# Softmax divisions, first differences and some low words of a fused attention, mix and channel kernel on other engines

## The chip, the cores and the metric

The kernel runs on one core of a Trainium2 chip. The metric is device microseconds for one execution of the whole program, from the first to the last instruction and the little that lies around them. A core has five engines with queues of their own, which meet through semaphores: TensorE (PE in the rows, its weight loads PEld), VectorE (DVE), ScalarE (ACT), GpSimd (POOL) and SyncE (SP), whose queue issues the DMAs here. Each engine takes its instructions strictly in order.

## The reference

Three stages in a chain, for a batch of 4, 576 positions, 8 heads of 64 channels (512 channels together):

```python
# 1 attention, per head: a window of 32 positions (plain, or with a stride of 4)
scores = where(mask, scale * q @ k.T, -1e9)
attn = exp(scores - max(scores));  attn = attn / (sum(attn) + 1e-9)
x = attn @ v
# 2 mix, with x_prev the row before
xk = mu_k * x + (1 - mu_k) * x_prev;  xr = mu_r * x + (1 - mu_r) * x_prev
k = relu(xk @ w_k);  y = sigmoid(xr @ w_r) * ((k * k) @ w_v)
# 3 channel
u = y + U, V mixing of y over positions
out = u + relu(u @ w_ch1) @ w_ch2
```

The weights arrive as 64-bit floats and are turned into 32-bit ones on the chip.

## The kernel before

**Attention** works on units: one unit is a pair of heads, one of two parts of the sequence and one batch element, 32 units in all. The first four units (`attend`) go alone, the other 28 in pairs (`attend2`). A unit has ten or eight windows of 32 queries by 64 keys. Its steps are: TensorE products `qk` (L606, L685) into `psS`; on VectorE mask and maximum (`low`, L546); on ScalarE the exponential with its sum, one instruction for each 64 columns (`exp`, L555); on VectorE the reciprocal of the sums (`inv`, L560 and L561); the division, which is a product with that reciprocal (`norm`, L566), **on GpSimd**, in one instruction for up to five groups of 64 columns; TensorE transposes (L637, L723); on ScalarE the copy `pts` out of PSUM; TensorE products with v (L649, L741); on ScalarE the copy into `x`.

**Mix** goes over eight half batches c = 0 to 7, each with four slices p of 128 channels. For each, `mix` makes the first difference `d` = x minus x of the position before (L356, **on GpSimd**) and from it `xk` (for c = 0) or `m` by one VectorE instruction (L778). For c = 0 the products are plain 32-bit matmuls (`r_row` L837, `k_row` L852, then L821), each of which the trace records twice; from c = 1 on each operand is split into a high word (copy on ScalarE, L361) and a low word (subtraction, L356 on GpSimd or L358 on VectorE), and each product is three fast matmuls (L824 to L826). A tile of a later c is 12 such matmuls; each c has 4 tiles for r, 8 for k and, for v, 4 of twice that length. PSUM has four banks `psM` for these accumulators and four `psS` for attention. The row of `r_row` for slice 3 ends the r sums of c = 0, which `sg` copies on ScalarE take out of the banks before `k_row` can go on.

**The weights of mix**, 20 pieces `wx` of 128x512, are loaded through a pool of four buffers `w`, and each is converted by one ScalarE instruction (L394) and four on VectorE (L395, L396, L398, L401); the last of them frees the buffer for the next load. Later `split_weight` makes `wh` and `wl` of each.

**The order** is not the order of the code. Each step is an `op` with an engine, an estimated duration and its reads and writes; `plan` passes forward and backward over all of them and gives each engine a fixed list. A duration or an engine that changes in one `op` can so move instructions on every engine. Where `plan` sees TensorE idle for over 0.6 us, it puts matmuls on zeros there (L1340), which take time as others do.

**After mix** the channel stage (from about 305 us on, L1058 to L1060 and L1137 to L1139) follows. The change has no instruction in it.

Of the kernel before, what the change touches and what calls it, by code (L numbers as in the profile page):

```python
# [76 lines left out]
FILL, FILL_FROM, FILL_NS, FILL_COLD = 0.6, 600.0, 0.453, 7000.0  # L77
PLAN_PRINT = None
PASSES = 24
EARLIER = {"d": -20}  # L80
RATE = 285.0

# [2 lines left out]
def tile_attention_mix_channel(  # L85
# [44 lines left out]
    def op(eng, ns, fn, r=(), w=(), more=100, lock=False, mode=None, size=0):  # L130

        o = Op()
        o.eng, o.ns, o.fn, o.r, o.w, o.more, o.lock, o.mode, o.size = eng, ns, fn, list(r), list(w), more, lock, mode, size
        ops.append(o)
# [217 lines left out]
    def sub(eng, n, out_, a, b, r, w, psum=False, fr=True):  # L352

        if eng == "POOL":
            t = 165 + 2.14 * n if fr else 110 + 1.93 * n
            op("POOL", t, lambda: nc.gpsimd.tensor_tensor(out=out_(), in0=a(), in1=b(), op=ALU.subtract), r, w, 40, lock=True)  # L356
        else:
            dve(n, lambda: nc.vector.tensor_tensor(out=out_(), in0=a(), in1=b(), op=ALU.subtract), r, w, two=True, psum=psum)  # L358
# [201 lines left out]
        nc.vector.tensor_scalar(sm[:, :n], sm[:, :n], 1e-9, None, op0=ALU.add)  # L560
        nc.vector.reciprocal(sm[:, :n], sm[:, :n])  # L561

    def norm(pr, d, sm, i, n, d_to=None):
        src = pr[:, d : d + n * KW].rearrange("p (w k) -> p w k", k=KW)
        dst = src if d_to is None else pr[:, d_to : d_to + n * KW].rearrange("p (w k) -> p w k", k=KW)
        nc.gpsimd.tensor_tensor(out=dst, in0=src, in1=sm[:, i : i + n].unsqueeze(2).to_broadcast([P, n, KW]), op=ALU.mult)  # L566

    LOW, EXP, NORM = 150, 330, 1.69 * KW

    def x_out(ov, q, part, b):  # L570

# [15 lines left out]
    def attend(u):  # L587
# [34 lines left out]
            for i in range(5):  # L622
                exp(pr(), i * KW, mn(), sm(), i)

        def norms():
            norm(pr(), 4 * KW, sm(), 4, 1, 5 * KW)
            norm(pr(), 0, sm(), 0, 5)

        op("DVE", 6 * LOW, lows, [(x,) for x in sc] + [("cst",)], [(pr,), (mn,)], 170)
        op("ACT", 5 * EXP, exps, [(pr,), (mn,)], [(pr,), (sm,)], 190, mode="exp")  # L630
        op("DVE", 260, lambda: inv(sm(), 5), [(sm,)], [(sm,)], 80, lock=True)
        op("POOL", 360 + 6 * NORM, norms, [(pr,), (sm,)], [(pr,)], 40, lock=True)
        yield

        def tr():
# [23 lines left out]
    def attend2(ua, ub):  # L659
# [33 lines left out]
        for e in range(2):  # L693
            first_, own = (ns - 4, 0) if e else (0, 4)
            base = e * ns * KW

            def lows(e=e, first_=first_, own=own, base=base):
                for i in range(4):
                    low(sc[e](), i * KW, pr(), base + (first_ + i) * KW, mk[i // 2], mn[e](), first_ + i)
                if nw == 10:  # L700
                    for f in range(2):
                        low(sc[f](), (4 + e) * KW, pr(), base + own * KW, mk[2], mn[e](), own, head(f))

            def exps(e=e, base=base):
                for i in range(ns):
                    exp(pr(), base + i * KW, mn[e](), sm[e](), i)

            kp, ks = [(pr, e)], [(sm[e],)]
            op("DVE", (4 + 2 * (ns - 4)) * LOW, lows, [(x,) for x in (sc if nw == 10 else sc[e : e + 1])] + [("cst",)], kp + [(mn[e],)], 170)
            op("ACT", ns * EXP, exps, kp + [(mn[e],)], kp + ks, 190, mode="exp")  # L710
            op("DVE", 260, lambda e=e: inv(sm[e](), ns), ks, ks, 80, lock=True)
            op("POOL", 180 + ns * NORM, lambda e=e, base=base: norm(pr(), base, sm[e](), 0, ns), kp + ks, kp, 40, lock=True)
        yield

        def to(i):
# [48 lines left out]
    def mix(c, p, which):  # L764
# [7 lines left out]
        d, kd = lambda: dt_[p // 2]()[:, p % 2 * HS : (p % 2 + 1) * HS], (dt_[p // 2], p % 2)  # L772
        if (c, p) not in dd:
            dd.add((c, p))
            sub("POOL", HS, d, lambda: x()[:, p, c0 : c0 + HS], xp, kx, [kd], fr=False)
        n = 4 * base + p
        out_, km = (lambda: xk0()[:, n * HS : (n + 1) * HS], (xk0, n)) if c == 0 else half_slot("m")
        dve(HS, lambda: nc.vector.scalar_tensor_tensor(  # L778
            out=out_(), in0=d(), scalar=mu_t[:, col + p : col + p + 1], in1=xp(), op0=ALU.mult, op1=ALU.add),
            kx + [kd, ("mu",)], [km] + ([("turn", "m")] if c else []), two=True)  # L780
        if c > 0:
            at(xk, 8 * base + p, 8 * base + 4 + p, out_, [km], "POOL")


    xk0 = Lazy([P, 8 * HS], F32, "x", "xk0", 2)
# [649 lines left out]
```

## Time and profile before

| | us |
|---|---|
| median of 3 runs | 750.92 (749.88 to 753.05) |
| the profiled execution | 750.69 |
| its span, first to last instruction | 748.8 |
| TensorE busy in the span | 733.4 |
| VectorE, ScalarE, GpSimd busy | 564.4, 393.1, 381.5 |

The prediction is made against the profiled execution: 750.69 us, 0.2 us below the median of the runs, and 1.9 us longer than its span. TensorE was busy for 98% of the span, so the first question is where the other 15.4 us are, and what of its busy time is matmuls on zeros. The views to read are the busy time by stretch, the timeline of TensorE with its waits, and for the other engines the timelines around those waits. In a timeline row the first number is the start, the second how long the row's instructions kept the engine busy from first start to last end, and "x8" their count; in brackets stands the idle time of the engine just before and what ended it.

### The profile page before, as it was taken

The page shows a single profiled execution, that of the slowest core. Times are in us where ns is not written, and L with a number is a line of the kernel's source. Part 1 is how long each engine was busy: PE and PEld are TensorE (multiplying, and loading weights), DVE is VectorE, ACT ScalarE, POOL GpSimd, SP SyncE. Part 2 cuts the span into 40 slices and gives each one's busy share as a digit, 9 for nine tenths or more (in the row PEclk, how much of TensorE's full clock was granted, in tenths as well). Part 3 has the DMA queues.
Part 4 walks back from the last instruction along what each step waited for, and adds up shares of the span by engine and source line. Part 5 has one row for each costly group of instructions (what it writes and reads, how often), then busy time and mean ns, then how long its engine had stood idle before and what let it go on. Part 6 is the DMA issues. An engine that isn't in the chain of part 4 may idle for free.

```text
span 748.8 us, 18318 instructions
## 1 busy us (share of the span) xinstructions
PE 733.4 (98%) x6920; PEld 675.5 (90%) x6920; DVE 564.4 (75%) x1335; ACT 393.1 (53%) x995; POOL 381.5 (51%) x400
## 2 busy tenths in 40 slices
PE   7899989999999999999999999999999999999998
PEld 5677989999999999999999898889888989898886
DVE  5999998899988754875778698785997765675532
ACT  5596785867676746473556345354454433343310
POOL 1332464646554644273766587444877645365500
PEclk9999999999999999999999999999999999999999
DMA  8877327767765550466733262133412212141001
GB/s 318 271 258 257 116 95 235 265 204 263 278 194 185 164 169 15 169 187 206 238 131 120 90 217 75 43 127 127 162 57 85 86 56 85 40 134 67 15 1 56
DMA packets 53223, 109.77 MB, mean 147 GB/s; under 512 B 5648, under 2 KB 15888, under 8 KB 53136
## 3 DMA queue, kind: packets, MB, share of 16 engines
q1 hardware_dynamic: 53136, 108.62, 43.4%
q8 instruction: 54, 0.88, 0.5%
q14 instruction: 33, 0.27, 0.1%
HBM read 86.05 MB, written 22.54 MB: 145 GB/s over the span
## 4 chain that ended last, share of the span: by engine, by line
PE 88%; DVE 5%; DMA 3%; ACT 2%; issue 1%; SPq 0%; POOL 0%; DVEq 0%; ACTq 0%; POOLq 0%
PE psM L824 10%; PE psM L826 10%; PE psM L825 10%; PE psS L1139 9%; PE psS L1137 9%; PE psS L1138 9%; PE psM L1058 8%; PE psM L1060 8%; PE psM L1059 8%; PE psS L741 2%; DMA w<-w1raw 2%; PE psM L821 1%; PE psS L685 1%; DVE wx L401 1%; DVE wx L398 1%; DMA raw<-qk 1%
## 5 line engine op out<-in xcount | busy, mean ns | idle before, releaser
L356 POOL TENSOR_TENSOR cl<-sums,ch 128x512 fp32r<-128x512 f32 x72 | 97.6, 1355 | 91.0 <-ACT ch L361 59.4
L361 ACT ACTIVATE ch<-sums 128x512 fp32r<-128x512 f32 (+1 forms) x104 | 57.7, 563 | 122.5 <-DVE sums L481 113.2
L1137 PE MATMUL psS<-hh,rh 128*128 128x512 f32 (+2 forms) x322 | 119.5, 371 | 0.4 <-ACT hh L1114 0.4
L1139 PE MATMUL psS<-hl,rh 128*128 128x512 f32 (+2 forms) x322 | 119.6, 371 | 0.0
L1138 PE MATMUL psS<-hh,rl 128*128 128x512 f32 (+2 forms) x322 | 119.2, 370 | 0.0
L824 PE MATMUL psM<-xk,wh 128*128 128x288 f32 x336 | 100.9, 300 | 0.0
L825 PE MATMUL psM<-xk,wl 128*128 128x288 f32 x336 | 99.1, 295 | 0.0
L826 PE MATMUL psM<-xk,wh 128*128 128x288 f32 x336 | 98.9, 294 | 0.0
L481 DVE TENSOR_TENSOR sums<-st 128x256 f32<-128x256 f32 (+1 forms) x144 | 86.6, 649 | 7.7 <-POOL cl L356 5.9
L356 POOL TENSOR_TENSOR cl<-st,ch 128x256 fp32r<-128x256 f32 x80 | 65.9, 840 | 48.5 <-PE psM L1060 34.9
L356 POOL TENSOR_TENSOR xk<-m,xk 128x288 fp32r<-128x288 f32 x56 | 52.4, 946 | 41.2 <-ACT xk L361 33.9
L1139 PEld LDWEIGHTS psS<-hl,rh 128*128 128x128 f32 x322 | 60.6, 188 | 11.6 <-DVE hl L1115 0.9
L1137 PEld LDWEIGHTS psS<-hh,rh 128*128 128x128 f32 x322 | 60.7, 188 | 10.4 <-ACT hh L1114 1.2
L1138 PEld LDWEIGHTS psS<-hh,rl 128*128 128x128 f32 x322 | 60.7, 189 | 9.4
L824 PE MATMUL psM<-k2s,wh 128*128 128x288 f32 x224 | 67.7, 302 | 0.0
L825 PE MATMUL psM<-k2s,wl 128*128 128x288 f32 x224 | 66.5, 297 | 0.0
L826 PE MATMUL psM<-k2s,wh 128*128 128x288 f32 x224 | 66.4, 296 | 0.0
L824 PEld LDWEIGHTS psM<-xk,wh 128*128 128x128 f32 x336 | 63.0, 187 | 0.7
L1095 DVE TENSOR_TENSOR ok<-ok,psM 128x256 f32<-128x256 f32 (+1 forms) x96 | 46.4, 504 | 22.4 <-PE psM L1060 20.0
L826 PEld LDWEIGHTS psM<-xk,wh 128*128 128x128 f32 x336 | 63.2, 188 | 0.0
L825 PEld LDWEIGHTS psM<-xk,wl 128*128 128x128 f32 x336 | 63.1, 188 | 0.1
L356 POOL TENSOR_TENSOR k2s<-k,k2s 128x288 fp32r<-128x288 f32 x49 | 43.0, 879 | 35.0 <-ACT k2s L361 32.5
(154 smaller groups left out, 2109.7 us busy)
## 6 DMA issues: line engine op xcount, KB each, us to landing
st<-w2f SPq DMA_DIRECT2D x96, 256.0 KB, 3.0
w<-w2raw SPq DMA_DIRECT2D x32, 512.0 KB, 5.2
w<-w1raw SPq DMA_DIRECT2D x20, 512.0 KB, 5.5
w2f<-w SPq DMA_DIRECT2D x32, 256.0 KB, 3.0
raw<-qk SPq DMA_DIRECT2D x16, 320.0 KB, 6.7
ytmp<-y SPq DMA_DIRECT2D x32, 144.0 KB, 2.2
yb<-ytmp SPq DMA_DIRECT2D x4, 1152.0 KB, 6.4
uf<-us SPq DMA_DIRECT2D x32, 144.0 KB, 1.8
```

The source lines that it names most:

```text
L356: op("POOL", t, lambda: nc.gpsimd.tensor_tensor(out=out_(), in0=a(), in1=b(), op=ALU.subtract), r, w, 40, lock=True)
L361: act(n, lambda: nc.scalar.activation(out_(), in_(), AF.Copy), r, w, psum, strided)
L481: dve(k * Q, lambda: nc.vector.tensor_tensor(out=q(sm_, n, k)(), in0=a(), in1=b(), op=op_), [(s1,), (s2,)], [(sm_, key)], two=True)
L824: nc.tensor.matmul(a, lhsT=wh, rhs=xh, start=start, stop=False)
L825: nc.tensor.matmul(a, lhsT=wl, rhs=xh, start=False, stop=False)
L826: nc.tensor.matmul(a, lhsT=wh, rhs=xl, start=False, stop=stop)
L1058: nc.tensor.matmul(a, lhsT=wh()[:, wi], rhs=xh()[:, ci], start=(k == 0), stop=False)
L1059: nc.tensor.matmul(a, lhsT=wl()[:, wi], rhs=xh()[:, ci], start=False, stop=False)
L1060: nc.tensor.matmul(a, lhsT=wh()[:, wi], rhs=xl()[:, ci], start=False, stop=(k == len(parts) - 1))
L1137: nc.tensor.matmul(a, lhsT=wh, rhs=xh, start=(j == 0 and e == 0), stop=False, skip_group_check=c0 > 0)
L1138: nc.tensor.matmul(a, lhsT=wl, rhs=xh, start=False, stop=False, skip_group_check=c0 > 0)
L1139: nc.tensor.matmul(a, lhsT=wh, rhs=xl, start=False, stop=(j == 7 and e == 1), skip_group_check=c0 > 0)
```

## The change

Three things move. The division of the first four units goes from GpSimd to VectorE (the same two instructions each); that of the other 28 goes to ScalarE, as one instruction for each 64 columns with the reciprocal as its scale (124 instructions in place of 28 on GpSimd). The first differences `d` of half batch 0 go from GpSimd to VectorE (4 instructions; those of the other half batches stay). The low words of `xk` of half batch 1 go from GpSimd to VectorE (8; the others stay).

```diff
+NORM_ENG = ("DVE", "DVE", "ACT", "ACT", "ACT")
+MIX_ENG = ("DVE", "POOL")
+XK_ENG = "DVE"
...
-    def norm(pr, d, sm, i, n, d_to=None):
+    def norm(eng, pr, d, sm, i, n, d_to=None):
+        if eng == "ACT":
+            for w in range(n):
+                to = (d if d_to is None else d_to) + w * KW
+                nc.scalar.activation(
+                    pr[:, to : to + KW], pr[:, d + w * KW : d + (w + 1) * KW], AF.Copy, scale=sm[:, i + w : i + w + 1])
+            return
...
-        nc.gpsimd.tensor_tensor(out=dst, in0=src, in1=sm[:, i : i + n].unsqueeze(2).to_broadcast([P, n, KW]), op=ALU.mult)
+        (nc.vector if eng == "DVE" else nc.gpsimd).tensor_tensor(out=dst, in0=src, in1=sm[:, i : i + n].unsqueeze(2).to_broadcast([P, n, KW]), op=ALU.mult)
...
+    def normed(u, n, k, fn, r, w):
+        eng = NORM_ENG[min(u // 2, len(NORM_ENG) - 1)]
+        if eng == "DVE":
+            op("DVE", 75 * k + 1.04 * n * KW, lambda: fn(eng), r, w, 80, lock=True)
+        elif eng == "POOL":
+            op("POOL", k * 180 + n * NORM, lambda: fn(eng), r, w, 40, lock=True)
+        else:
+            op("ACT", 60 + n * 245, lambda: fn(eng), r, w, 140)
...
-        op("POOL", 360 + 6 * NORM, norms, [(pr,), (sm,)], [(pr,)], 40, lock=True)
+        normed(u, 6, 2, norms, [(pr,), (sm,)], [(pr,)])
...
-            sub("POOL", HS, d, lambda: x()[:, p, c0 : c0 + HS], xp, kx, [kd], fr=False)
+            sub(MIX_ENG[min(c, 1)], HS, d, lambda: x()[:, p, c0 : c0 + HS], xp, kx, [kd], fr=False)
...
-            at(xk, 8 * base + p, 8 * base + 4 + p, out_, [km], "POOL")
+            at(xk, 8 * base + p, 8 * base + 4 + p, out_, [km], XK_ENG if c == 1 else "POOL")
```

`plan` then orders everything anew. In the rows below `pr,sm<-pr,mn` is the exponential, `pts` the copy of transposed scores, `wx<-w` the first step of a weight's conversion, `x` the attention's result.

ScalarE, the first instructions after its table load, before:

```order
L555 ACTIVATE pr,sm<-pr,mn 128x64 x5
L394 ACTIVATE wx<-w_100 128x512
L555 ACTIVATE pr,sm<-pr,mn 128x64 x5
L361 ACTIVATE pts<-psS 128x384
L394 ACTIVATE wx<-w_135 128x512
```

The same place after:

```order
L558 ACTIVATE pr,sm<-pr,mn 128x64 x5
L397 ACTIVATE wx<-w_100 128x512
L364 ACTIVATE pts<-psS 128x384
L558 ACTIVATE pr,sm<-pr,mn 128x64 x5
L364 ACTIVATE x_95<-psS 128x320
L397 ACTIVATE wx<-w_135 128x512
```

The exponentials of the second unit now stand behind `pts` of the first.

TensorE between the row of r for slice 1 and the one for slice 3 (`xk,wx 128x288 x4` is one row of r; `zero` is matmuls on zeros; `pts,raw` the products with v; `raw` qk), before:

```order
L1340 MATMUL psM<-zero 128x224 x5
L837 MATMUL psM<-xk_325,wx 128x288 x4
L649 MATMUL psS<-pts,raw 64x32 x20
L685 MATMUL psS<-raw 32x64 x32
L837 MATMUL psM<-xk_325,wx 128x288 x4
L1340 MATMUL psM<-zero 128x224 x5
L837 MATMUL psM<-xk_325,wx 128x288 x4
```

The same place after:

```order
L1358 MATMUL psM<-zero 128x224 x13
L855 MATMUL psM<-xk_302,wx 128x288 x8
L655 MATMUL psS<-cst_t,pr 128x128 x3
L1358 MATMUL psS<-zero 128x512 x2
L759 MATMUL psS<-pts,raw 64x32 x20
L703 MATMUL psS<-raw 32x64 x32
L1358 MATMUL psM<-zero 128x224 x28
L855 MATMUL psM<-xk_302,wx 128x288 x4
```

The rows of slices 1 and 2 now come ahead of the fourth unit's products with v, and before the last row of r there are 28 matmuls on zeros instead of five.

VectorE after the first reciprocal, before:

```order
L560 TENSOR_SCALAR sm<-sm 128x5
L561 RECIPROCAL sm<-sm 128x5
L546 ISA pr,mn<-psS,cst_t 128x64
L546 ISA mn 128x1
L546 ISA pr,mn<-psS,cst_t 128x64
```

The same place after:

```order
L563 TENSOR_SCALAR sm<-sm 128x5
L564 RECIPROCAL sm<-sm 128x5
L398 TENSOR_SCALAR wx<-wx 128x512
L575 TENSOR_TENSOR pr<-pr,sm 128x64
L575 TENSOR_TENSOR pr<-pr,sm 128x320
L399 TENSOR_SCALAR wx<-wx 128x512
```

The two divisions of the first unit stand inside a weight's conversion, ahead of the second unit's maxima.

## Rows read from the trace of the kernel before

**Rows 1.** By stretch: length; PE, PEld, DVE, ACT, POOL busy; clock, DMA share, GB/s.

```profile
40.00:72.40 32.40, 30.78 (x386) 23.73 (x384) 31.23 (x94) 25.84 (x76) 8.02 (x11) 1.00 0.74 247
...
105.00:700.00 595.00, 593.84 (x5383) 558.83 (x5380) 454.22 (x1010) 311.42 (x755) 338.68 (x346) 1.00 0.44 144
...
106.00:107.00 1.00, 1.00 (x10) 0.99 (x5) 0.89 (x9) 1.00 (x4) 1.00 (x2) 0.50 0.89 233
```

**Rows 2.** Timeline of TensorE from 35 to 75 us: start, busy, instruction.

```profile
35.74 2.21 PE L837 MATMUL psM<-xk,wx 128*128 128x288 f32 x8 [0.49 <-DVE xk L778]
...
42.23 6.57 PE L852 MATMUL psM<-xk,wx 128*128 128x288 f32 x26
...
50.12 7.93 PE L821 MATMUL psM<-xk,wx 128*128 128x288 f32 x32
57.88 0.60 PE L723 MATMUL psS<-cst_t,pr 128*128 128x128 f32 x4
...
59.17 1.14 PE L741 MATMUL psS<-pts,raw 64*64 64x32 f32 x64 [0.22 <-ACT pts L361]
...
61.24 8.03 PE L821 MATMUL psM<-k,wx 128*128 128x288 f32 x32
...
69.88 1.63 PE L821 MATMUL psM<-k,wx 128*128 128x288 f32 x6
72.44 2.91 PE L821 MATMUL psM<-k,wx 128*128 128x288 f32 x11 [0.93 <-DVE wx L401]
```

**Rows 3.** Timeline of TensorE around 102 us.

```profile
101.33 0.29 PE L825 MATMUL psM<-xk,wl 128*128 128x288 f32 x1
101.46 0.29 PE L826 MATMUL psM<-xk,wh 128*128 128x288 f32 x1
103.65 1.37 PE L741 MATMUL psS<-pts,raw 64*64 64x32 f32 x80 [1.90 <-ACT pts L361]
...
106.02 0.61 PE L824 MATMUL psM<-k2s,wh 128*128 128x288 f32 x1
...
108.80 0.29 PE L824 MATMUL psM<-k2s,wh 128*128 128x288 f32 x1
```

**Rows 4.** Timeline of ScalarE, the second unit's exponentials and the first `pts`.

```profile
9.62 0.35 ACT L555 ACTIVATE pr<-pr,mn 128x64 f32<-128x64 f32 x1 [1.15 <-DVE mn L546]
...
11.43 0.49 ACT L361 ACTIVATE pts<-psS 128x384 f32<-128x384 f32 x1
```

**Rows 5.** Timeline of VectorE, second reciprocal and `xk` of slice 3.

```profile
12.71 0.17 DVE L560 TENSOR_SCALAR sm<-sm 128x5 f32<-128x5 f32 x1
...
13.17 0.43 DVE L395 TENSOR_SCALAR wx<-wx 128x512 f32<-128x512 f32 x1
...
15.18 0.23 DVE L546 CUSTOM_DVE_ANT_0 pr<-psS,cst_t 128x64 f32<-128x64 f32 x1 [1.13 <-PE psS L606]
...
35.17 0.51 DVE L778 SCALAR_TENSOR_TENSOR xk<-d,mu_t,x 128x288 f32<-128x288 f32 x1
35.60 0.69 DVE L398 SCALAR_TENSOR_TENSOR wx<-w,wx 128x512 int32<-128x512 int32 x1
```

**Rows 6.** Timeline of VectorE, instructions that lasted longer beside GpSimd's.

```profile
19.88 1.23 DVE L395 TENSOR_SCALAR wx<-wx 128x512 f32<-128x512 f32 x2
...
24.11 0.89 DVE L395 TENSOR_SCALAR wx<-wx 128x512 f32<-128x512 f32 x1
...
26.36 1.09 DVE L401 SCALAR_TENSOR_TENSOR wx<-w,wx 128x512 int32<-128x512 int32 x1
...
51.15 2.37 DVE L398 SCALAR_TENSOR_TENSOR wx<-w,wx 128x512 int32<-128x512 int32 x2
```

**Rows 7.** A line on ScalarE: duration ns min/median/max of copies of 128x160.

```profile
L361 ACT ACTIVATE us<-w x4: 323/334/338, 231.1 to 232.4; 128x160 fp32r<-128x160 f32 x4
```

**Rows 8.** GpSimd's groups up to 72.4 us: busy us, mean ns, idle before.

```profile
L356 POOL TENSOR_TENSOR d<-x 128x288 f32<-128x288 f32 x8 | 7.2, 904 | 16.7 <-ACT x L361 16.7
...
L566 POOL TENSOR_TENSOR pr<-pr,sm 128x320 f32<-128x320 f32 x4 | 3.3, 834 | 0.3
```

More of the change, by code (lines that the diff above doesn't have):

```diff
@@ L623, in exps, with norms @@
                 exp(pr(), i * KW, mn(), sm(), i)
-        def norms():
-            norm(pr(), 4 * KW, sm(), 4, 1, 5 * KW)
-            norm(pr(), 0, sm(), 0, 5)
+        def norms(eng):
+            norm(eng, pr(), 4 * KW, sm(), 4, 1, 5 * KW)
+            norm(eng, pr(), 0, sm(), 0, 5)
         op("DVE", 6 * LOW, lows, [(x,) for x in sc] + [("cst",)], [(pr,), (mn,)], 170)
@@ L711, in attend2 @@
             op("DVE", 260, lambda e=e: inv(sm[e](), ns), ks, ks, 80, lock=True)
-            op("POOL", 180 + ns * NORM, lambda e=e, base=base: norm(pr(), base, sm[e](), 0, ns), kp + ks, kp, 40, lock=True)
+            normed(ua, ns, 1, lambda eng, e=e, base=base: norm(eng, pr(), base, sm[e](), 0, ns), kp + ks, kp)
         yield
```

## The prediction

> **What bounds the kernel now.** I first read the busy time by stretch. From 105 to 700 us TensorE works 593.84 of 595.00 us at the full granted clock [rows 1], and the change takes no instruction off TensorE. So nothing can be gained there; what a change of the other engines can give or take lies before 105 us, or is a wait that it newly makes. Then I read TensorE's timeline from 35 to 75 us [rows 2]: its waits are short, and each ends on an engine that the change touches. Third, the one large wait further on [rows 3]. Fourth, what VectorE and ScalarE do before the last row of r [rows 4, 5], because that row waits for `xk` on VectorE, and VectorE is full: 31.23 of 32.40 us from 40 to 72.4 us [rows 1].
>
> Two places therefore hold what there is to win or lose.
>
> **Place 1, the start.** After the last row of r (35.74 us) TensorE still has room before c = 1. I count it from the time after qk of the fifth and sixth units (42.23 us) [rows 2]: 42.23 + 6.57 = 48.80 to 50.12 is 1.32 us, 57.88 + 0.60 = 58.48 to 59.17 is 0.69, 61.24 + 8.03 = 69.27 to 69.88 is 0.61, 69.88 + 1.63 = 71.51 to 72.44 is 0.93. Some of it is idle time and some matmuls on zeros, and all of it, 3.55 us, could be taken up if TensorE came later. The new order puts three matmuls on zeros into this stretch, 0.45 us as an upper bound from the 0.61 us that seven of them cost above.
>
> **Place 2, the wait at 101.75 us.** TensorE stands 1.90 us for `pts`, which is late on ScalarE [rows 3]. [...] So this place costs 1.90 + 1.18 = 3.1 us.
>
> **The change part by part.**
>
> *Divisions of the first four units on VectorE.* No row shows such a product on VectorE. The nearest is `xk`, 128x288 with two tensors from SBUF: the next instruction starts 35.60 - 35.17 = 0.43 us behind it [rows 5]. For 128x320 that makes 0.48, and for 128x64 I take 0.17, as for the 128x5 instruction [rows 5]: 0.65 us a unit. The bounds are 0.43, if the small one costs nothing, and 0.9, a little more than GpSimd's 0.834 for the large one [rows 8].
>
> *First differences of c = 0 on VectorE.* 128x288 again: 0.43 us each, with 0.51, the whole duration of that row, as upper bound.
>
> *What GpSimd no longer disturbs.* VectorE's instructions last longer beside GpSimd's. Up to the last row of r three places show it: two of L395 in 1.23 us for 0.86, one in 0.89 for 0.43, one L401 in 1.09 for 0.69 [rows 5, 6]. Together 0.37 + 0.46 + 0.40 = 1.23 us, all beside instructions that now leave GpSimd. The lower bound of the relief is these 1.23 us; the upper, that each moved GpSimd instruction gives back its whole time: half of the eight `d`, 3.6, and the large divisions, 3.3 [rows 8], 6.9 us. I take the lower, since it is what the rows show.
>
> [...] The rows above show delays of 0.37 to 0.46 us beside GpSimd instructions of 0.8 to 0.9, so half of that at most. [...]
>
> *The last row of r.* From the second reciprocal (12.71) to the end of `xk` of slice 3 (35.60) VectorE takes 22.89 us now. I counted both orders between these two instructions. The new one has 4 `d` (1.72), 3 divisions (1.95), three more steps of weights (two at 0.62, one at 0.40) and one more reciprocal with its addition (0.40): +5.71. Off go the relief, 1.23, and the idle 1.13 us at 15.18 [rows 5], where VectorE waits for qk of the third unit and will now have work: 22.89 + 5.71 - 2.36 = 26.24 us. The start of the stretch moves too. ScalarE now does `pts` of unit 1 ahead of the second unit's exponentials; `pts` can't end before 11.43 + 0.49 = 11.92, because the transpose stays where it was, and the five exponentials took from 9.62 to about 11.4, 1.75 us [rows 4]. So they end at 13.67, and the reciprocal starts at 13.8 instead of 12.71. `xk` of slice 3 is then there at 13.8 + 26.24 = 40.04, and the last row of r at 40.2 instead of 35.74: 4.45 us later. Queued behind the exponentials on ScalarE are `x` and the second weight, which wait with them; behind the divisions on VectorE are all weights.
>
> *Sum of place 1.* 4.45 late, 3.55 of it taken up, 0.45 of zeros: 1.35 us lost. This needs the last weight to come no later than TensorE. VectorE is 4.45 us late at that row but has done three steps of weights and a reciprocal more, 2.04, so 2.4 us in terms of weights; from there to the last weight the order adds two low words and a reciprocal and takes off one `m`, +0.8, and a pair at 51.15 that took 2.37 us for some 1.3 [rows 6] shows relief of 1.1, with some more at others, 2.4 in all as an estimate. The last weight is so 0.8 us later, inside the 1.35. SP's queue has the same loads in nearly the same places, each freed by the last step of an earlier weight, and follows VectorE.
>
> *Low words of half batch 1 on VectorE.* Eight at 0.43, 3.4 us, two of them before the last weight. VectorE has no room from 72 to 103 us either, but GpSimd's divisions and low words there go at the same time. I count it as nothing for the sum; the cover is this relief, and without it the weights' low words come up to 2.6 us later and TensorE waits so long.
>
> *Divisions of the other 28 units on ScalarE.* 124 instructions. A copy of 128x160 takes 0.334 us [rows 7], one of 64 columns no longer; by columns alone it would be 0.13. I take 0.25, nearer the upper, since part of an instruction's time does not shrink. 124 x 0.25 = 31 us (16 to 41) on an engine with over 350 us idle. TensorE sees it only through `pts`, `k2s` and `rt` behind it in the queue; each group of divisions also waits for VectorE's reciprocal, and these stand behind that wait.
>
> *Place 2 after.* The pair of units that waits at 101.75 is now served earlier: its transposes stand after the third k tile less four products instead of late in the seventh, and VectorE and ScalarE have had less time to fall behind. Stepping through ScalarE's list there, `pts` comes just in time for the 12 matmuls between transposes and products, with 0.3 us to spare, but the next pair's maxima and divisions now stand inside the k tiles, and the last `k2s` comes about 1 us after TensorE wants it at the v tiles. What is left there can be anything from 0 to 3.1 us, or more (third case). I take 2.0, one wait of 1.1 with a short fall of the clock: 1.1 us won.
>
> **Sum.** 750.69 + 1.35 - 1.1 = 750.9 us. Measurements of this kernel can tell about 0.5%, 3.75 us, from no change; this is within it. Its own range is 747.5 to 754.5: the divisions at 0.43 to 0.9 move place 1 by -0.7 to +0.8, `d` up to +0.3, the three others of place 1 by about 1, and place 2 by -2.0 to +1.1.
>
> **The rivals.**
>
> [...] If the relief is half way between 1.23 and 6.9, 4.1 us, the last row of r comes at 37.3, 1.6 late; 1.6 - 3.55 + 0.45 = -1.5. If the wait at 101.75 goes too, -3.1: 746.1 us. For it: GpSimd's busy share before 72 us falls to a fraction. Against: the traced delays are small, and VectorE gets 5.7 us of work. It decides once the relief is over 3 us. That this is faster by more than 0.5% needs both halves.
>
> *ScalarE's queue, slower.* Divisions of eight or ten times 0.25 us stand between `k2s` and `rt` in each round of attention, where TensorE asks for a k tile every 12 x 0.13 = 1.6 us. If ScalarE comes later than the slack, TensorE stands as it does now [rows 3], at 3.1 us a time. It decides from a delay of `pts` beyond those 12 matmuls. Of the 14 rounds, two such waits beside the one in the sum would give 750.69 + 1.35 + 6.2 = 758.2. For it: the divisions wait for VectorE inside the queue. Against: after 105 us TensorE has but 1.16 us of waits now [rows 1], with the same chain over GpSimd.
>
> *Nothing of place 2 changes.* The start is taken up as said and an equal wait stays: 750.69 + 1.35 = 752.0, also no change that can be told.
>
> **Chances.** Forecast 0.50, lock 0.22, queue 0.20, equal wait 0.08. Faster by over 0.5% (below 746.9): the lock and a little of the forecast's lower end, 0.24. Slower (above 754.4): the queue and 0.04 of the forecast, 0.24. Within: 0.52. The range that leaves half of each rival out goes from 745.0 to 757.5.
>
> **What would show it.** Right: the last row of r starts near 40 us with idle time ahead of it despite 28 matmuls on zeros; from 42 to 75 us no wait is left; the first matmul of c = 1 is 1 to 2 us later than now, less the attention products that have moved ahead of it; a division of 128x320 on VectorE takes about 0.48 and one of 64 columns on ScalarE about 0.25 us; near 95 us there is no wait for `pts`, and a short one at the first v tiles of c = 1. Wrong: the row of r near 36 us, VectorE's weights finishing before 72, or several waits of over 1 us between 105 and 300 us that end on ScalarE.

## The result and the profile after

| | before | after |
|---|---|---|
| median of 6 runs, us | 750.40 (749.2 to 753.05) | 754.68 (754.12 to 755.94) |
| ratio, 95% interval | | 1.0056 (1.0038 to 1.0075) |
| span of the profiled execution | 748.8 | 752.1 |
| VectorE, ScalarE, GpSimd busy | 564.4, 393.1, 381.5 | 559.7, 420.4, 343.6 |

The change makes the kernel 4 us slower. GpSimd gave up 37.9 us and ScalarE took 27.3; VectorE is even busy for 4.7 us less. The busy time by stretch, of after (as [rows 1]; columns: stretch, length, then PE, PEld, DVE, ACT, POOL busy with counts, granted clock, DMA share, GB/s), says where the loss is:

```profile
40.00:72.40 32.40, 30.73 (x387) 23.86 (x386) 29.34 (x97) 29.00 (x92) 3.54 (x5) 1.00 0.78 261
105.00:260.00 155.00, 150.69 (x2147) 147.38 (x2146) 131.20 (x411) 120.87 (x389) 69.38 (x82) 1.00 0.62 205
105.00:700.00 595.00, 590.14 (x5310) 555.09 (x5309) 447.81 (x990) 328.75 (x829) 323.02 (x324) 1.00 0.43 141
```

From 105 us on TensorE stands 4.86 us where it stood 1.16 [rows 1], and 4.31 of them lie before 260 us. Its timeline after has these waits (answers to [rows 2, 3]):

```profile
34.05 3.39 PE L1358 MATMUL psM<-zero 128*128 128x224 f32 x28
39.03 2.21 PE L855 MATMUL psM<-xk,wx 128*128 128x288 f32 x8 [1.59 <-DVE xk L796]
...
56.91 2.21 PE L839 MATMUL psM<-xk,wx 128*128 128x288 f32 x8 [1.55 <-ACT rt L899]
...
97.37 1.37 PE L759 MATMUL psS<-pts,raw 64*64 64x32 f32 x80 [0.85 <-ACT pts L364]
...
145.31 0.40 PE L842 MATMUL psM<-k2s,wh 128*128 128x288 f32 x1 [0.41 <-DVE k L904]
...
155.88 1.37 PE L759 MATMUL psS<-pts,raw 64*64 64x32 f32 x80 [1.79 <-ACT pts L364]
...
160.35 0.40 PE L842 MATMUL psM<-k2s,wh 128*128 128x288 f32 x1 [0.70 <-issue]
...
206.35 0.40 PE L842 MATMUL psM<-xk,wh 128*128 128x288 f32 x1 [1.09 <-DVE y L919]
```

The first two places moved as foreseen in kind: the last row of r came late, the wait near 102 us shrank from 1.90 to 0.85 us (now at 97 us), and no half clock (a granted clock of 0.50, as before had [rows 1]) followed: it was 1.00 from 97 to 102 us. All rows from 145 us on are new. A ledger puts sizes to it. At the start of each round of products with v I took the difference in time between the kernels, less 0.133 us for each fast matmul of mix (0.133 is their pitch: in before, ten of them start from 108.80 to 110.00 us) that after had done more; where it had done fewer, the same is added:

```
start, before   start, after   matmuls of c >= 1 done   after is late by
120.52          114.48         240 / 204                -1.24
138.99          134.56         360 / 336                -1.23
154.58          155.88         456 / 456                +1.30
192.31          193.55         696 / 684                +2.84
210.79          214.97         816 / 816                +4.18
228.79          232.16         924 / 924                +3.37
```

So the start and the place near 102 us together won 1.2 us, the stretch from 135 to 215 us lost 5.4, and a wait of 0.59 us that only before has at 213 us (0.8 with its restart) leaves 3.3 to 3.4. Nothing changes after that.

The chain of work that ended last, from the page of before and then of after, shares of the span by engine:

```profile
PE 88%; DVE 5%; DMA 3%; ACT 2%; issue 1%; SPq 0%; POOL 0%; DVEq 0%; ACTq 0%; POOLq 0%
```

```profile
PE 71%; DVE 16%; ACT 6%; DMA 4%; issue 2%; SPq 0%; POOL 0%; DVEq 0%; ACTq 0%
```

Before, the chain ran through TensorE from 103 us nearly to the end. After, it runs from 20 to 206 us through VectorE, ScalarE and transfers; of the 101 us from 105 to 206 us VectorE has 54, transfers 20 and ScalarE 16. So VectorE may set the pace there although it is busy for only 131.2 of 155 us. A chain through many short waits is no proof of that; the experiments test it.

### The profile page after: what moved, and what is told of

It is laid out like the page before. It is cut to its first block, busy times and chain, and to the rows that moved or that the text cites. A ratio compares the mean times of both kernels' runs of the same rounds, so it can differ in the third digit from the quotient of the medians.

```text
span 752.1 us, 18403 instructions
## 1 busy us (share of the span) xinstructions
PE 732.5 (97%) x6934; PEld 674.8 (90%) x6934; DVE 559.7 (74%) x1355; ACT 420.4 (56%) x1119; POOL 343.6 (46%) x352
## 4 chain that ended last, share of the span: by engine, by line
PE 71%; DVE 16%; ACT 6%; DMA 4%; issue 2%; SPq 0%; POOL 0%; DVEq 0%; ACTq 0%
PE psS L1157 9%; PE psS L1155 9%; PE psS L1156 9%; PE psM L1076 8%; PE psM L1078 8%; PE psM L1077 8%; PE psM L842 6%; PE psM L844 5%; PE psM L843 5%; ACT pr L558 1%; DVE pr L549 1%; DVE m L796 1%; DVE wl L361 1%; DVE w L404 1%; DVE w L401 1%
## 5 line engine op out<-in xcount | busy, mean ns | idle before, releaser
L359 POOL TENSOR_TENSOR xk<-m,xk 128x288 fp32r<-128x288 f32 x48 | 43.7, 926 | 68.3 <-ACT xk L364 51.3
L359 POOL TENSOR_TENSOR k2s<-k,k2s 128x288 fp32r<-128x288 f32 x49 | 44.7, 913 | 49.9 <-ACT k2s L364 48.1
```

## The experiments

In all of them `before` ran on the same chip, and a ratio is to it, with its 95% interval.

### The parts alone and in pairs

The three parts of the change were moved one by one. "Start" in the table means the first four units' divisions together with the first differences of c = 0:

| start on VectorE | later divisions on ScalarE | low words on VectorE | ratio |
|---|---|---|---|
| | yes | | 1.0021 (1.0001 to 1.0042) |
| | | yes | 0.9996 (0.9980 to 1.0013) |
| yes | | | 1.0082 (1.0062 to 1.0102) |
| yes | yes | | 0.9993 (0.9977 to 1.0009), again 1.0008 (0.9987 to 1.0029) |
| yes | | yes | 1.0016 (1.0001 to 1.0030) |
| | yes | yes | 1.0097 (1.0072 to 1.0122) |
| yes | yes | yes | 1.0056 (1.0038 to 1.0075), again 1.0059 (1.0039 to 1.0079) |

**Later divisions alone.**

```diff
-NORM_ENG = ("DVE", "DVE", "ACT", "ACT", "ACT")
-MIX_ENG = ("DVE", "POOL")
-XK_ENG = "DVE"
+NORM_ENG = ("POOL", "POOL", "ACT")
+MIX_ENG = ("POOL", "POOL")
+XK_ENG = "POOL"
```

> Only the divisions of the units from the fifth on go to ScalarE; the first four stay on GpSimd, as do the first differences of x and the low words of mixes. Theory (ScalarE's time): the TensorE waits of 4.3 us that the changed kernel shows between 105 and 260 us come from the 27 us more of ScalarE work, so they are here too, near 145 and 155 us above all, while the start costs nothing (last row of r near 35.7 us as before, not 39.0) and the wait near 101 us is as in the changed kernel: about 753.8 us, 1.0045 of before. Rival (low words): the waits come from half batch 1's low words on VectorE; then they are missing here and the kernel is faster than before by the 2.2 us that the place near 101 us gave: about 748.2 us. Rival (order): the waits belong to the one order that was planned for the changed kernel, and this kernel has waits of its own, anywhere from 747 to 756 us, at other places.

751.96 us, 1.0021: neither the 753.8 of the theory nor the 748.2 of the first rival. No engine makes TensorE wait between 105 and 260 us; its 1.6 us of idle time there have no releaser in the trace. So 27 us more on ScalarE do not by themselves make the waits.

**The change without divisions on ScalarE.**

```diff
-NORM_ENG = ("DVE", "DVE", "ACT", "ACT", "ACT")
+NORM_ENG = ("DVE", "DVE", "POOL")
```

> No division on ScalarE: those of the first four units stay on VectorE and the others go back to GpSimd; first differences of x and half batch 1's low words on VectorE as in the changed kernel. Theory (ScalarE's time): no wait beyond 0.6 us between 105 and 260 us; the start costs its 0.9 us; the place near 101 us keeps some wait: 749 to 752 us. Rival (low words): the 4.3 us of waits between 105 and 260 us stay: about 754 us. Rival (order): any time from 748 to 756 us, with the waits at new places.

752.23 us, near the 749 to 752 of the first theory, with waits for an engine of 0.31 and 0.52 us at other places. One wait of 1.88 us, without a releaser, it did not foresee.

**The change without low words on VectorE**, measured twice.

```diff
-XK_ENG = "DVE"
+XK_ENG = "POOL"
```

> The changed kernel with half batch 1's low words of mixes back on GpSimd; divisions and first differences of x stay where the change puts them. The kernel with the divisions of later units on ScalarE alone showed no TensorE wait on an engine between 105 and 260 us. Theory (sum of three parts): the start costs 1 to 1.4 us, the place near 101 us gains 2, and the waits near 145, 155 and 206 us come with the low words and the order that they force; without these words they go: about 751.0 us, 1.001 of before. Rival (ScalarE's time at a full VectorE): the waits stay at 145 and 155 us, since the divisions and the first differences are still there: about 754.5 us, as the changed kernel.

> The changed kernel without its low words on VectorE, once more: 0.9993 of before, 0.998 to 1.001; no TensorE wait for an engine over 0.5 us between 72 and 260 us, as in its first profile. If that profile was a lucky one, waits of 1 us and more appear here.

Both times as fast as before, with 0.3 us of waits for an engine from 72 to 260 us in the first profile, 0.3 in the second. Against the full change the low words cost about 4 us here, their new order included; without the two other parts (second row) they cost nothing.

**The start alone.**

```diff
-NORM_ENG = ("DVE", "DVE", "ACT", "ACT", "ACT")
-XK_ENG = "DVE"
+NORM_ENG = ("DVE", "DVE", "POOL")
+XK_ENG = "POOL"
```

> Only the start is changed: the divisions of the first four units and the first differences of x on VectorE; the later divisions and all low words stay on GpSimd. Theory (start): the last row of r comes 3 to 3.5 us late, 12 more products of zeros and the use of later room make that 0.9 to 1.5 us at 82 us, and the wait near 101 us may stay (1.9 us and half clock): 751.3 to 752.5 us, 1.001 to 1.003 of before. Rival (start costs nothing): the later room takes all of it: 750.4 us, 1.000.

Far slower than either expected. Waits of TensorE, 72.4 to 260 us (columns: engine and line, what it waited for, us in total, times, longest):

```profile
PE psM L842 <- DVE w L399: 2.2, 1, 2.2
PE psM L842 <- DVE mn L549: 0.8, 1, 0.8
PE psS L759 <- ACT pts L364: 0.7, 2, 0.5
...
```

and, before that stretch, one of 2.88 us for `sg` on ScalarE, up to 43.73 us. With the later divisions on ScalarE as well, the same start costs nothing (0.9993).

**The start undone.**

```diff
-NORM_ENG = ("DVE", "DVE", "ACT", "ACT", "ACT")
-MIX_ENG = ("DVE", "POOL")
+NORM_ENG = ("POOL", "POOL", "ACT")
+MIX_ENG = ("POOL", "POOL")
```

> The changed kernel with its start undone: the divisions of the first four units and the first differences of x back on GpSimd; half batch 1's low words stay on VectorE and the later divisions on ScalarE. Theory (start): 1 to 1.5 us less than the changed kernel in the same runs, with the last row of r near 35.7 us. Rival (start costs nothing): the same as the changed kernel within 0.5 us. If the low words make the waits near 145 and 155 us, these are here.

Slower by 3 us, not faster. Its waits, 105 to 260 us:

```profile
PE psS L703 <- issue: 3.3, 1, 3.3
PE psM L843 <- issue: 1.5, 1, 1.5
PE psM L842 <- DVE y L919: 1.0, 1, 1.0
```

From 164.5 us, still within the wait of 3.3 us, to 171.3 us the granted clock was 0.50. By the ledger this kernel is 1.2 us late at the round of products with v ahead of this place and 7.0 at the next one: 5.8 of the 6.4 us that its profile loses in all lie here, and not in a wait for VectorE. The two large waits have no releaser; the last section comes back to them.

**Divisions only.**

```diff
-MIX_ENG = ("DVE", "POOL")
-XK_ENG = "DVE"
+MIX_ENG = ("POOL", "POOL")
+XK_ENG = "POOL"
```

> Only the divisions move: the first four units' to VectorE, all others' to ScalarE; first differences of x and all low words stay on GpSimd. Beside the kernel with the first differences on VectorE too (0.9993 of before) it prices these differences. Theory (VectorE's time decides the start): 1.7 us less of VectorE before the last row of r, so the row comes near 37.5 us instead of 39.2 and the whole is 0.5 to 1.5 us faster: 0.998. Rival (GpSimd's differences at 0.9 us are as late, and share its queue): no change or slower, 0.9995 to 1.002, with rows of r waiting for d.

1.0079 (1.0051 to 1.0106), slower than both expected: four first differences more on GpSimd, and TensorE waits four times for `pts`, 3.5 us, from 72 to 260 us.

**Low words alone.**

```diff
-NORM_ENG = ("DVE", "DVE", "ACT", "ACT", "ACT")
-MIX_ENG = ("DVE", "POOL")
+NORM_ENG = ("POOL", "POOL", "POOL")
+MIX_ENG = ("POOL", "POOL")
```

> Only half batch 1's low words of mixes move to VectorE; all divisions and the first differences stay on GpSimd. It is the one combination of the three parts not yet run. If the low words cost VectorE's 3.5 us whatever else is moved, it stands 0.4 to 0.6% above before, as the changed kernel stands above the one without low words. If the parts can't be priced one by one, since each gives another planned order, anything from 0.999 to 1.010.

The wait near 102 us is gone without any division having moved, and 1.0 us of waits for `pts` and VectorE near 155 to 160 us has come. The time is that of before, so the first expectation, a price of 0.4 to 0.6% whatever else is moved, is wrong.

**The full change again**, without an edit.

> The changed kernel once more, unaltered, beside the others of these runs: 754.7 us, 1.0056 of before. Where the wait near 155 us for pts and the wait near 206 us for y belong to the order, they are here again within 0.5 us of 1.79 and 1.09 us; where they come of how transfers happen to fall in one execution, they differ by more.

The wait for `pts` near 156 us is 1.79 us once more, so it belongs to the order; that for `y` at 206 us is missing, so the order alone does not make it. In this second profile the chain lies on TensorE from 98 to 136 us, leaves it for VectorE and ScalarE up to 157, and then lies on TensorE again, which has 79 of the 101 us from 105 to 206 us. TensorE's idle time from 105 to 260 us is 2.70 us here and was 4.31 in the first, and the ledger loses 3.8 us from 135 to 215 us in place of 5.4: so much two profiles of one kernel differ. The parts have no prices that add up: low words cost 4 to 6 us beside divisions on ScalarE (without the start mostly by the one wait without a releaser), and nothing or less than nothing without them.

### ScalarE's time, or its place in the queue

**Divisions on ScalarE left out**, the order of all engines kept.

```diff
-            for w in range(n):
+            for w in range(0):
```

> The changed kernel with its order kept on every engine, but the divisions on ScalarE (units from the fifth on) are left out, so attention of these units is not divided by its sum. ScalarE has 27 us less to do and nothing else moves. Theory (ScalarE's time): the waits at 145 and 155 us (0.41 and 1.79 us) go, as their queue of ScalarE is shorter by 1.3 to 2.6 us just ahead; the wait at 206 us, which ends with a transfer of y, stays or shrinks: 751.5 to 753 us if it stays, 750.5 us if all go. Rival (order): the waits are due to where the order puts the instructions and the transfers, not to ScalarE's time: no change, 754 to 755 us.

1.0035 (1.0020 to 1.0050). The wait for `pts` near 154 us falls from 1.79 in both profiles of the full change to 0.30. TensorE's idle time from 105 to 260 us, 2.69 us, is no less than the 2.70 of the second profile. Taking away all of the 27 us wins some 1.6 us, and the intervals still overlap; it does not win the loss.

**The same divisions on GpSimd, same order.**

```diff
-        if eng == "ACT":
+        if eng == "":
```

> The changed kernel with its order kept, but the divisions of the units from the fifth on are run by GpSimd, in the same place of the program, as one instruction for 4 or 5 columns of 64. ScalarE has 27 us less. Theory (ScalarE's time): like the kernel without these divisions, plus what GpSimd's 0.75 to 0.85 us for each 4 or 5 and its queue cost the transposes behind it: 751 to 754 us, and faster than the changed kernel. Rival (order): 754 to 756 us, the waits at the same places, 145, 155 and 206 us.

1.0111 (1.0094 to 1.0128), slower than both expected: `pts` is late three times between 72 and 260 us, 4.0 us, and half clock follows the wait of 2.10 at 100.78. In this order ScalarE is the better place for them.

**`pts` ahead of the sigmoid.** ScalarE's timeline of after, at the wait of 1.79 us:

```profile
152.71 1.28 ACT L890 ACT_TABLE_LOAD   x1
154.01 1.16 ACT L890 ACTIVATE sg<-sg 128x1152 f32<-128x1152 f32 x1
155.08 0.75 ACT L364 ACTIVATE pts<-psS 128x512 f32<-128x512 f32 x2
```

```diff
+        order = plan()
+        acts = [o for o in order if o.eng == "ACT"]
+        sg = [o for o in acts if o.mode == "sig"][2]
+        k = acts.index(sg)
+        pts = [o for o in acts[k + 1 : k + 3] if o.kind == "pts"]
+        order = [o for o in order if o not in pts]
+        k = order.index(sg)
+        order[k:k] = pts
-        for o in plan():
+        for o in order:
```

> The changed kernel with one swap in ScalarE's queue: at the third sigmoid (near 153 us) the two copies of pts go ahead of the table load and the sigmoid instead of behind them; nothing else moves on any engine. In the changed kernel the transposes for pts end at 152.5 us, ScalarE then spends 2.35 us on table load and sigmoid, copies pts at 155.08 and TensorE waits 1.79 us for it, in both profiles taken. Theory (place in the queue): the wait goes, y comes 0.75 us later, which nobody on TensorE waits for: 1.8 us less than the changed kernel, ratio 1.0033 against its 1.0056 to 1.0059. Rival (ScalarE has too much to do before): the wait shrinks by no more than 0.5 us or comes back behind the sigmoid: 1.005 to 1.006.

The wait is gone from that place and the time is the same, 1.0068 (1.0041 to 1.0095). Its waits, 105 to 260 us:

```profile
PE psM L842 <- DVE y L919: 1.4, 2, 1.2
PE psS L703 <- issue: 1.1, 1, 1.1
PE psM L842 <- DVE k L904: 0.9, 2, 0.6
PE psS L759 <- ACT pts L364: 0.8, 1, 0.8
```

4.2 us again, elsewhere. A wait that comes back when it is taken away is a sign that something slower stands behind it.

### VectorE's chain

**One VectorE step less.** One step in the conversion of each of the 32 pieces of the channel stage's weights (L398 in the kernel before, L401 in the changed one) is left out of the full change.

```diff
-    def cv_bits(raw, n, xt_=None):
+    def cv_bits(raw, n, xt_=None, times=1):
...
-        dve(n, lambda: nc.vector.scalar_tensor_tensor(
-            out=xi(), in0=words()[1], ..., op0=ALU.bitwise_and, op1=ALU.bitwise_or),
+        dve(n, lambda: [nc.vector.scalar_tensor_tensor(
+            out=xi(), in0=words()[1], ..., op0=ALU.bitwise_and, op1=ALU.bitwise_or) for _ in range(times)],
...
-        x, kx = cv_bits(raw, CW)
+        x, kx = cv_bits(raw, CW, times=0)
```

> The changed kernel with its order kept on every engine, but one VectorE step in the decoding of the second stage's weights (the one that puts sign and exponent back, 0.78 us each, 20 of them from 105 to 206 us, 32 in all) is left out, so those weights and the outputs that hang on them are wrong. VectorE has 15.6 us less to do between 105 and 206 us. Theory (VectorE's chain): the chain that ended last runs from 20 to 206 us through VectorE and what waits on it, not through TensorE; with that work gone TensorE's waits in this stretch, 4.3 us before, shrink to under 1.5 us, and the whole comes to 1.001 to 1.002 of before. Rival (places in the queues and transfers): the waits for pts near 155 us, for y's store near 206 us and those without a releaser stay, 1.005 to 1.006, as after the swap of pts.

0.9993 (0.9980 to 1.0007). From 105 to 260 us VectorE is busy 114.80 us in place of 131.20, and TensorE 153.96 in place of 150.69:

```profile
105.00:260.00 155.00, 153.96 (x2174) 150.96 (x2173) 114.80 (x391) 124.66 (x406) 67.28 (x83) 1.00 0.64 209
```

From 135 to 215 us the ledger loses 1.8 us, where the two profiles of the full change lose 5.4 and 3.8. All waits for `pts`, `k` and `y` are gone from the stretch; what is left has no releaser:

```profile
PE psM L842 <- issue: 0.7, 2, 0.4
PE psS L703 <- issue: 0.3, 1, 0.3
```

**The same step twice, in the kernel before** (`times=2`; order kept).

> The kernel before with the same VectorE step of the second stage's weights done twice (the second leaves the value as it is), the order of all engines kept: VectorE has 16.2 us more to do between 105 and 206 us. In the kernel before the chain runs through TensorE from 103 us on, with VectorE busy 138.0 of 155 us from 105 to 260. Theory (VectorE's chain): VectorE's room of 17 us is eaten, the chain moves to it, and TensorE gets 3 us and more of waits there that it had not: 1.004 to 1.012 of before. Rival (VectorE has room enough): no wait over 0.5 us more, 1.000 to 1.002.

1.0254 (1.0228 to 1.0281), more than expected: 18.6 us for 32 steps of 0.78 us, 25 us. The step in the kernel before:

```profile
L398 DVE SCALAR_TENSOR_TENSOR w<-w,w 128x512 int32<-128x512 int32 x32 | 24.8, 778 | 0.2
```

The stretch in the kernel before, and then in this one:

```profile
105.00:260.00 155.00, 154.41 (x2231) 151.70 (x2228) 138.00 (x432) 109.22 (x335) 83.96 (x102) 0.99 0.67 222
```

```profile
105.00:260.00 155.00, 141.82 (x1989) 137.07 (x1979) 145.64 (x419) 96.52 (x296) 74.68 (x89) 0.99 0.64 209
```

Its waits there:

```profile
PE psS L741 <- ACT pts L361: 5.9, 6, 1.8
PE psM L824 <- DVE k L886: 2.9, 2, 1.5
PE psS L685 <- issue: 2.1, 2, 1.9
PE psM L824 <- DVE sg L863: 1.3, 2, 0.9
...
```

Of the waits that a late VectorE makes, the largest part (5.9 of 13.1 us) is booked to `pts` on ScalarE, which is only the next in line. VectorE's 17 us of idle time in the kernel before were hardly room: they lie in waits inside its queue (4.2 us for `rt` on ScalarE, 3.5 for TensorE's sums), and of 25 us more work 18.6 reached the end, 0.75 for each. That price holds for this step in this order: the low words alone, 3.6 us more on VectorE ahead of 105 us, cost nothing.

**VectorE relieved.** The copies of r's tiles out of PSUM on ScalarE, in the kernel before and in the one with low words alone.

```diff
-            if whole:
+            if True:
                 copy(HS, lambda: sig()[:, o, :], lambda: acc()[:, :HS], [(acc,)], [(sig, o)], psum=True)
```

> The kernel before with VectorE relieved instead of loaded: the copies of r's tiles out of the accumulators (450 ns each, 20 of them up to 260 us, 8.9 us) go to ScalarE, and the order is planned anew. Theory (VectorE's chain sets the pace up to 206 us, 0.8 us of TensorE wait for each us more): less of VectorE can win back only the waits that stand, the 1.90 us and the half clock near 102 us: 747.5 to 750 us, 0.996 to 0.999 of before. Rival (ScalarE's queue): the copies stand in front of pts and rt on ScalarE and TensorE waits for these as often: 1.000 to 1.006.

> Half batch 1's low words on VectorE (0.9996 of before, with the wait near 102 us gone) and the same copies of r's tiles on ScalarE, so that VectorE ends with less to do than before (8.9 us fewer, 3.6 us more up to 260 us). Theory (VectorE's chain): the 1.0 us of waits for pts and VectorE between 155 and 160 us go too: 748 to 750 us, 0.996 to 0.999. Rival (each new order has waits of its own): 1.000 to 1.006.

1.0117 (1.0097 to 1.0137) and 1.0055 (1.0038 to 1.0073), both outside what the theory gave; the first is outside its rival too, the second is as its rival had it. All waits of the first, from 72.4 to 260 us:

```profile
PE psS L685 <- issue: 7.8, 6, 2.5
```

No engine is waited for any more, as VectorE's chain would have it, but TensorE stands 7.8 us without a releaser, and three of the six gaps are followed by half clock (3.4, 1.7 and 1.7 us lost, as 1 less the granted clock, added over single microseconds). The second still waits from 72.4 to 260 us, 1.4 us for `mn` on VectorE, 1.0 for `pts` and 1.0 without a releaser, and 3.0 us for `us` on VectorE behind 260 us. So relieving VectorE by a new order did not pay; only with the order kept did it.

**More transfers.** The change without low words, each store of a decoded weight done twice.

```diff
+    w2x = [tc.dram_tile([P, 2 * CW], F32, name=f"w2x{i}") for i in range(16)]
...
-        dma(P * CW * 4, lambda: nc.sync.dma_start(w2f[i][:, j * CW : (j + 1) * CW], x()), kx, [("w2f", i, j)])
+        dma(P * CW * 4, lambda: [nc.sync.dma_start(t[i][:, j * CW : (j + 1) * CW], x()) for t in (w2x, w2f)], kx, [("w2f", i, j)])
```

> The same kernel, with each store of a decoded piece of the second stage's weights (256 KB) done twice, the second to a place that nobody reads: 8 MB more of transfers, most of them between 105 and 260 us, and the same order on all compute engines. It asks what TensorE's idle time inside runs of small matmuls, for which no releaser is seen, comes from. Theory (crowded transfers): these gaps (0.78 us in one place in this kernel) grow to 2 us and more in several places, in slices in which the transfers' share is near 1.0, and other waits on transfers come with them: 1.003 to 1.010. Rival (the gaps belong to the instruction sequence): they stay at 0.5 to 1 us, and any loss shows as waits on transfers of weights or y.

1.0051 (1.0029 to 1.0073), some 3 to 4 us for the doubled stores. The wait without a releaser is 1.4 us, once, so it did not grow in several places as the theory had it; 3.4 us of waits for `k`, `pts`, `y` and `k2s` came with it. So transfers can make TensorE wait through the other engines as well.

No kernel measured here is faster than before by more than its interval.

## Why the prediction was right and wrong

The forecast was 750.9 us, no change that can be told, with 747.5 to 754.5 as its own range; measured were 754.68, 4 us above before.

**What held.** The groups of after, with shapes apart (busy us, mean ns of one, idle before):

```profile
L570 ACT ACTIVATE pr<-pr,sm 128x64 f32<-128x64 f32 x124 | 31.9, 336 | 2.5 <-DVE sm L564 2.4
...
L361 DVE TENSOR_TENSOR xk<-m,xk 128x288 fp32r<-128x288 f32 x8 | 3.5, 447 | 0.0
...
L575 DVE TENSOR_TENSOR pr<-pr,sm 128x320 f32<-128x320 f32 x4 | 2.0, 493 | 0.1
...
L361 DVE TENSOR_TENSOR d<-x 128x288 f32<-128x288 f32 x4 | 1.8, 454 | 0.0
...
L575 DVE TENSOR_TENSOR pr<-pr,sm 128x64 f32<-128x64 f32 x4 | 0.9, 218 | 0.0
```

A unit's divisions took VectorE 0.66 us from start to start (0.65 said), a difference 0.36 to 0.49 (0.43), a division on ScalarE 0.22 by what ScalarE gained (27.3 / 124; 0.25 said).

- *The reciprocal.* It started at 13.58 us, counted as in the prediction from the addition ahead of it (13.8 said).
- *The last row of r.* 39.03 us (40.2 said): the instruction behind `xk` started at 38.89, a stretch of 25.31 us instead of 26.24, so with the other terms as measured the relief from GpSimd was about 2.1 us and not 1.23. It waits 1.59 us despite its 28 matmuls on zeros. In the second profile the stretch took 26.4 us, since 1.1 us of VectorE's idle time stayed, and the row came at 41.01.
- *The last weight.* 72.79 against 72.29 us, 0.5 late (0.8 said).
- *Sum of place 1.* The first matmul of c = 1 started at 82.83 us instead of 79.28; less 2.31 us for the products with v and qk that had moved ahead of it, it was 1.2 us late (1.35 said). That the sum came so near is luck: the row of r was 1.2 us less late than said, and the forecast that no wait is left from 42 to 75 us failed by 1.55 us for `rt` at 56.91. In the second profile this matmul was 2.3 us late; the second `raw` had landed 0.9 us later there than in the first.
- *The first rival* ("lock" in the chances). The relief of 2.1 us is below its point of 3 us, and a third of the prediction's upper bound, 6.9 us, with which the whole time of the moved instructions would come back.

**Mis-sized: place 2.** Won were 2.5 us (from 1.2 late to 1.2 ahead), not 1.1. The wait near 95 us, said to go, stayed with 0.85 us, while the wait said for the v tiles and the half clock did not come. The place had also cost more than the 3.1 us of the sum: at half clock its 64 qk matmuls took 1.07 us up to the next matmul, and after the change 0.78. The 1.18 us in that sum is an estimate from [rows 1, 3]: at a granted clock of 0.50, the 12 matmuls from 106.02 to 108.80 us took 2.78 us, which at the pitch of 0.13 ahead of the wait would be 1.60. Up to 135 us the change is thus a gain of 1.2 us, where the sum had a loss of 0.25.

**Failed: "Low words of half batch 1 on VectorE ... I count it as nothing for the sum".** The cover named was GpSimd's relief up to 103 us. It held up to there: the eight low words ended at 86.4 us, and at 135 us TensorE was still 1.2 us ahead. The loss came later, 4.6 us from there to 3.4 behind. Without the low words on VectorE it is not there (0.9993 and 1.0008), so beside the two other parts they cost 4 us. But leaving them out also gave a new order, and no run parts their time from the order that came with them.

The step behind it is the first paragraph's: for the stretch from 105 us, in which TensorE worked 593.84 of 595.00 us, it named waits that the change might newly make, and the sum has no term for them. In its place the runs showed that VectorE's queue sets TensorE's time there. In the changed order 16.4 us less of VectorE's work brought the kernel back to 0.9993; in the kernel before 25 us more of it cost 18.6.

**The second rival had the sign, not the cause.** It said ScalarE's queue and, against it, "after 105 us TensorE has but 1.16 us of waits now". Waits for `pts` did come, one of 1.79 us. But leaving ScalarE's divisions out won some 1.6 us of the 4, taking `pts` out of its bad place nothing, and relieving VectorE in the same order all. No rival looked at VectorE as the bound after 105 us.

**Open.** Why the start alone and the low words beside ScalarE's divisions cost 6 to 7 us, while the start with those divisions costs nothing. For the second, most of the loss is one wait for no engine and the half clock around it, so VectorE's queue is not the cause in every slow order. Each setting gets its own order, and what was tested tells the pace-maker of one of them, not the rule by which an order gets slow.

## What to carry over

An engine in order with 11% idle time may have hardly any room (of 25 us more for VectorE, 18.6 came out at the end); double one of its steps, without another change, and see what the neighbour pays before work is moved to it. When a wait is booked to the engine next door, take work off the engines behind it, with the order kept, before queues are reordered: what comes back elsewhere was not the cause. Where a planner reorders everything, parts of a change have no prices that add up, so the whole is to be measured as one. And a wait without a releaser is to be looked at by its place in the instruction stream, as the next section does.

## What the runs showed of the hardware

TensorE can stand inside a run of small matmuls with no engine to wait for. In the kernel before with r's copies on ScalarE, TensorE's timeline:

```profile
102.82 1.37 PE L741 MATMUL psS<-pts,raw 64*64 64x32 f32 x80
104.12 0.79 PE L685 MATMUL psS<-raw 64*32 64x64 f32 x57
107.37 0.44 PE L685 MATMUL psS<-raw 64*32 64x64 f32 x7 [2.46 <-issue]
```

The qk run of 64 stops after 57. In the gap, from 105 to 106 us, one transfer of instructions stands in the view of the DMA queues (kind: packets, MB, share), behind a microsecond in which data held 76% of the DMA engines:

```profile
q8 instruction: 1, 0.02, 6.0%
q1 hardware_dynamic: 4, 0.00, 1.2%
```

On the page of after that queue has 54 transfers of 0.88 MB, 16.3 KB each. The 6934 matmuls of after and as many weight loads are 13868 instructions, 257 for each of these transfers.

The places of the waits fit such a number. Number all of TensorE's rows in a trace by their start: matmuls, weight loads and the semaphore rows of its sequencer. The 19 profiles of this case show 35 waits of TensorE without a releaser, of 0.21 to 3.33 us. After each one TensorE goes on at a number that is 193 or 194 above a multiple of 256, 1.1 to 1.6 us behind the end of a transfer on q8. Five of them:

```
kernel                           goes on at   wait   number   less 256s   q8 ended before
before                           213.45       0.59   5826     194         1.46
after                            160.35       0.70   4290     194         1.61
no divisions on ScalarE          160.05       1.88   4289     193         1.42
start undone                     166.18       3.33   4289     193         1.32
before, r's copies on ScalarE    107.37       2.46   2753     193         1.28
```

By number and place I take these for waits for more instructions; that is inferred, and no run took the transfers on q8 away. Why one comes late at these places and in time at most others is not shown. A round of products with v and qk has up to 320 instructions with its weight loads, in 2.4 us (after, from 78.69 us), more than the 257 for each transfer, and 23 of the 35 waits lie within its qk. In the kernel in which no engine is waited for, they (7.8 us) and the half clock behind three of them (6.8 us) cover what its span lost, 12.0 us.

Half clock does not follow every wait of a length. Waits of 1.90 us before [rows 3], 1.88 with the step doubled and 3.33 with the start undone came with 0.50, and so did two of 0.89 and 1.11 us, three microseconds apart, with divisions only; 1.79 in after, 1.88 without divisions on ScalarE, and 2.88 and 2.22 with the start alone did not, with 1.00 around them.
